# Attention into a leaky-ReLU MLP: a small memset behind GpSimd's copies, and an earlier place for one copy among VectorE's weight sums

## The chip, the cores and the metric

The kernel runs on one core of a Trainium2 chip. The metric is device time of one launch in microseconds (us). The engines are TensorE (PE, with its weight loads as PEld), VectorE (DVE), ScalarE (ACT), GpSimd (POOL) and SyncE (SP), each with a queue of its own that it works off in order; DMAs are issued from the queues of POOL (loads of the inputs) and SP (transposes and stores).

## The reference

```python
scores = scale * np.matmul(q, k.transpose(0, 1, 3, 2))      # q, k, v: 8 x 12 x 448 x 64, scale 1/8
scores = scores - np.max(scores, axis=-1, keepdims=True)
attn = np.exp(scores)
attn = attn / (np.sum(attn, axis=-1, keepdims=True) + 1e-09)
attn_out = np.matmul(attn, v)
x = attn_out.transpose(0, 2, 1, 3).reshape(3584, 768)
h = x @ w_in                                                # 768 x 2048
g = np.maximum(0.01 * h, h)
out = g @ w_out                                             # 2048 x 768
```

## The kernel before

**Pairs.** Attention is done for two heads at a time: pair u of 48, six pairs to a batch. A pair's q, k and v are loaded by DMA as bf16 into tiles `fq`, `fk`, `fv`, two pairs to a load, and copied by POOL (`cast`, L162 to L172): q and k into `qkb`, v into `v`, 112x512 each. For pairs up to 14, PE turns q and k (`transposes`, L248) into PSUM and DVE copies the result to `qkT` (L261); from pair 15 on (`NPE`) a DMA transpose from SP's queue does it (`turn`, L238). Then come four score chunks per pair (`scores`, L272, two matmuls each), an exponential on ACT for each chunk (L281), and `rows` (L755): 32 small matmuls (L764), the reciprocal of the sums (L770), and a scaled copy to `x` (L771), which is transposed to `xT` by DMA, in a few cases by PE (L318) with a copy by DVE (L319).

**The MLP.** The tokens are cut into seven blocks, of 640 first and 512 or so after that. Both weight products use a two-by-two scheme with seven products instead of eight, so sums of weight blocks are needed once and sums of data blocks for each token block. `mix_w_in` (L386, L390) and `mix_weights` (L364, L366, L369, L372) are generators: each `next` puts one sum of 128x768 bf16, with both inputs and the output in SBUF, into DVE's queue. `mix_weights` makes 16, in two halves of eight: for two pieces L364 then L366, then twice L369, then twice L372. L364 and L366 make `w_mix` 1 and 0, L369 changes `w_out_sb` in place, and L372 makes `w_mix` 2. `mix_h` (L435, L436) makes the same kind of sums of the hidden layer, `mix_x_part` (L415) of `xT`.

**Order.** [...] After the first batch's attention (`first`), `head` does the first 448 tokens' hidden layer, and `neck` (L609) the next 192, in eight groups; the function `after(x)` behind each group puts `mix_h` and some sums of `mix_weights` into DVE's queue. `second(0)` then does the first block's output product: `block_pair` (L518) yields after every four matmuls (L535), with DVE's work on `h` (L547, L552) and on the output (L540 copies a product from PSUM, L543 adds one). Into the gaps, `place` (L842) puts bursts of three score chunks and `rows`, by a small model of the engines' times in the program. In `second(0)` each second step also takes one more `next` of `mix_weights` if any is left. Later blocks are `hidden(i)` (L438) and `second(i)`, between which POOL's copies and load issues are given out by `advance` (L733); in the first phase this is done by `feed` (L822), from pair 12 on.

The product in `block_pair` that first reads `w_mix` is its third one, with `w_mix` 0 (t2 in the code); `w_out_sb` as changed by L369 is read by the fourth (t1), `w_mix` 1 by the fifth (t3), and `w_mix` 2 by the last (t4).

**Pair 14** is the last that PE turns. At the end of `neck` its turned q and k lie in a PSUM slot and wait for the copy L261:

```python
        after(len(ms) - 1)                       # neck: the last group's sums
...
    model["free"][id(slots[0])] = model["now"] + 1.5
    model["now"] += 0.45
    transposes(NPE - 1, next_slot()[:, 0])       # pair 14, ahead of second(0)
    to["pe"] += 1
    second(0)
```

`gate` is a 128x2 tile, written once at the start and used for nothing later.

Of the kernel before, what the change touches and what calls it, by code (L numbers as in the profile page):

```python
# [16 lines left out]
def kernel(  # L17
# [9 lines left out]
    nc = tc.nc  # L27
# [4 lines left out]
    HP = H // 2  # L32
# [34 lines left out]
    slots = [ps_s.tile([P, 2, 512], F32, name=f"sc{i}") for i in range(3)]  # L67

    def next_slot():

        slots.append(slots.pop(0))
        return slots[-1]

    def next_bank():

        banks.reverse()
        return banks[1]
# [17 lines left out]
    def place_of(t):  # L95
        return (t + NX - cuts[3]) % NX
# [65 lines left out]
    def cast(u, parts=(0, 1, 2), by=nc.gpsimd.tensor_copy):  # L162
        if u >= NU:
            return
        for x in parts:
            f = raw[u].pop(x)
            if x < 2 and u not in qk_sb:
                qk_sb[u] = cast_pool.tile([SC, 2, NSC, 2, D], BF16, name="qkb")
            if x < 2:
                by(qk_sb[u][:, x].rearrange("p so h d -> p h so d"), f)  # L170
            else:
                by(v_sb[u % NV][:, :, :, :D], f)  # L172

    w_steps = []
    for i in range(4):
# [26 lines left out]
    gate = const_pool.tile([P, 2], F32)  # L202
# [7 lines left out]
    def stay_warm(n):  # L210

        ps = next_slot()
        for _ in range(n):
            nc.tensor.matmul(ps[:, 0, :P], warm[:, :P], warm[:, :P], start=True, stop=True)
# [10 lines left out]
    def both(o, i):  # L225
        nc.scalar.copy(o[:, 0], i[:, 0])
        fast(o[:, 1], i[:, 1])

    cast(0, (1,), both)
    cast(0, (0,), both)  # L230


    x_t = {}

    NPE = HP + 9
# [8 lines left out]
    def turn_tile(bank):  # L244
        bank = next_bank() if bank is None else bank
        return bank.bitcast(BF16)[:, :2 * S].rearrange("p (i s) -> p i s", i=2)

    def transposes(u, bank=None):  # L248
        if u >= min(NPE, NU):
            return  # L250
        for parts in ((1,), (0,)) if u == 0 else ((0, 1),):
            tr = turn_tile(bank)
            for i in parts:
                for so in range(NSC):
                    nc.tensor.transpose(  # L255
                        tr[:, i, ts(so, SC)], qk_sb[u][:, i, so], ident[:SC, :SC]
                    )
            if u == 0:
                stay_warm(3 if parts == (1,) else 5)
            at = slice(parts[0], parts[-1] + 1)  # L260
            (nc.scalar.copy if u == 0 and parts == (1,) else nc.vector.tensor_copy)(  # L261
                qkT[u % NQ][:, :QL].rearrange("p (i s) -> p i s", i=2)[:, at], tr[:, at]
            )
# [73 lines left out]
    def settle():  # L337
        while late:
            expo(*late.pop(0))
# [88 lines left out]
    def mix_h(i, m):  # L428

        at = spots(i)[1]  # L430
        step = [max(1, at[-1][y] - at[0][y]) for y in range(2)]
        one, two = (slice(at[0][y], at[-1][y] + 1, step[y]) for y in range(2))
        lo, hi = slice(m, m + 2), slice(MH + m, MH + m + 2)
        t = h.rearrange("p m (c t) -> p m c t", t=P)
        nc.vector.tensor_sub(h_mix[:, lo, :len(at)], t[:, lo, one], t[:, lo, two])  # L435
        nc.vector.tensor_add(t[:, lo, two], t[:, lo, two], t[:, hi, two])  # L436
# [172 lines left out]
    def neck(outs):  # L609

        n = cuts[1] - HEAD
        at = place_of(HEAD)
        ms = [x + y for x in range(0, MH, 2) for y in (0, MH)]
        held = {}

        def part2(m, kks):
            fresh = m not in held
            if fresh:
                held[m] = next_bank()
            for j in range(2):  # L620
                for kk in kks:
                    nc.tensor.matmul(
                        held[m][:, j * n:(j + 1) * n], w_in_sb[:, kk, ts(m + j, P)], xT[:, kk, at:at + n],
                        start=(fresh and j == 0 and kk == 0), stop=(kk == KD - 1), skip_group_check=True,
                    )

        assert all(u == need[1] - 1 for u, _ in owed_x), owed_x
        def after(x):
            if x % 2:
                mix_h(0, ms[x - 1])  # L630
            for _ in range((1, 1, 1, 1, 1, 1, 2, 2)[x]):
                next(outs)

        for m in ms[:2]:
            part2(m, range(KD - 1))
        yield 4 * (KD - 1) * n / 2400, False
        for x, m in enumerate(ms):
            if x < 2:
                assert rows_done >= need[1], rows_done
                settle_x()  # L640
                part2(m, (KD - 1,))
                if x:
                    after(x - 1)
            else:
                part2(m, range(KH))
                after(x - 1)
                yield 2 * KH * n / 2400, False
                part2(m, range(KH, KD))
            nc.scalar.activation(
                h[:, m:m + 2, HEAD:cuts[1]], held.pop(m)[:, :2 * n].rearrange("p (m t) -> p m t", m=2), AX.Prelu, alpha=0.01  # L650
            )
            settle()
            yield 2 * (KH if x > 1 else 1) * n / 2400, True
        after(len(ms) - 1)

    def supply(u):

        for what, n in {0: [('qk', 2), ('qk', 3), ('v', 1), ('v', 2), ('load', 6)], 1: [('qk', 4), ('v', 3), ('load', 8)], 2: [('qk', 5), ('v', 4), ('w', 1)], 3: [('qk', 6), ('v', 5), ('w', 1)], 4: [('qk', 7), ('v', 6), ('load', 10)], 5: [('qk', 8), ('v', 7), ('w', 1), ('load', 12)]}[u]:
            if what == "qk":
                cast(n, (0, 1), fast if n in (2, 3) else nc.gpsimd.tensor_copy)  # L660
            elif what == "v":
                cast(n, (2,))
            elif what == "load":
                load(n)
            else:
                load_w(n)
# [132 lines left out]
    def settle_x(now=None):  # L799
        while owed_x and (now is None or owed_x[0][1] <= now and model["free"].get(id(slots[0]), 0.0) <= now + 0.05):  # L800
            model["free"][id(slots[0])] = model["now"] + 1.0
            model["now"] += 0.3
            x_transposes(owed_x.pop(0)[0], next_slot()[:, 0])
# [36 lines left out]
    model = {"now": 0.0, "act": 0.0, "free": {}, "ready": {}}  # L840
# [89 lines left out]
    for steps, aims, cost in ((head(ins, outs), early, 0.55), (neck(outs), goals, 0.5)):  # L930
        groups = 0
        base = len(early) if aims is goals else 0
        for used, full in steps:
            model["now"] += used
            if full:
                groups += 1
                model["act"] = max(model["act"], model["now"]) + cost
            soon = base + sum(x <= groups + 1 for x in aims) - done if full else 0
            done += place(0, base + sum(x <= groups for x in aims) - done, soon, first=True, lazy=True, full=full, keen=NU if aims is goals or groups > 13 else 0)
    settle()  # L940
    assert done == len(early) + len(goals), (done, chunk, rows_done)
    assert to["pe"] == NPE - 1, to
    model["free"][id(slots[0])] = model["now"] + 1.5
    model["now"] += 0.45
    transposes(NPE - 1, next_slot()[:, 0])
    to["pe"] += 1
    second(0)
    for _ in ins:
# [40 lines left out]
```

## Time and profile before

| | |
|---|---|
| median of 3 runs | 397.86 us (397.19 to 398.31) |
| the profiled execution | 398.14 us, span 396.4 us |
| PE busy | 380.4 us, 96% of the span |
| DVE busy | 236.8 us, 60% |
| ACT busy | 265.0 us, 67% |
| POOL busy | 140.0 us, 35%, 222 instructions |
| chain that ended last | PE 86%, DVE 5%, DMA 3%, issue 2%, ACT 2%, POOL 1% |

Times in the views are microseconds from the start of the span. A timeline line gives start, duration, engine, source line, operation, output tile and inputs, the shape, and in square brackets the idle time ahead of it and what ended it. Some neighbouring instructions of one kind are merged (x2, x32); back to back instructions overlap by some 0.06 to 0.08 us in the records. In the page, the row of busy tenths and that of the clock (PEclk) cut the span into 40 slices of 9.9 us.

### The profile page before, as it was taken

The numbers are of one execution on the slowest core, as the hardware profiler recorded it, in microseconds if no ns is written. First come the engines' busy times: TensorE is split into PE (matmuls) and PEld (weight loads), VectorE is DVE, ScalarE is ACT, GpSimd is POOL, SyncE is SP. The second block draws the span as 40 slices with busy tenths as digits, with TensorE's granted clock in tenths as the row PEclk, the third lists the DMA queues.
The fourth block names the chain that finished last, engine by engine and source line by source line (L and its number), as shares of the span: only waits on it lengthen the run. The fifth ranks groups of instructions, "written<-read, shape, count | busy, mean of one in ns | idle before, by whom it ended". The sixth has DMA issues, their size and how long they took to land.

```text
span 396.4 us, 10009 instructions
## 1 busy us (share of the span) xinstructions
PE 380.4 (96%) x4086; PEld 259.6 (65%) x4086; DVE 236.8 (60%) x494; ACT 265.0 (67%) x391; POOL 140.0 (35%) x222
## 2 busy tenths in 40 slices
PE   7899998759999999999999999999999999999996
PEld 3565656626659755697556975569755696568854
DVE  3653637973655854658448584464845656465754
ACT  6988874616587777677676776767767688708700
POOL 8897732934255321470216502265022200000000
PEclk9999999959999999999999999999999999999999
DMA  9999999994999918896398943989529520322023
GB/s 137 199 201 204 176 203 141 129 116 73 167 143 172 132 36 155 145 182 67 60 145 150 170 57 60 174 150 134 68 58 166 113 58 2 80 63 67 2 69 91
DMA packets 93246, 46.75 MB, mean 118 GB/s; under 512 B 51856, under 2 KB 89872, under 8 KB 93200
## 3 DMA queue, kind: packets, MB, share of 16 engines
q0 software_dynamic: 38224, 22.58, 45.2%
q1 hardware_dynamic: 54912, 23.50, 31.0%
q8 instruction: 32, 0.52, 0.6%
q14 instruction: 14, 0.11, 0.1%
q10 hardware_dynamic: 64, 0.02, 0.0%
HBM read 45.61 MB, written 11.01 MB: 143 GB/s over the span
## 4 chain that ended last, share of the span: by engine, by line
PE 86%; DVE 5%; DMA 3%; issue 2%; ACT 2%; POOL 1%; DVEq 0%; POOLq 0%; ACTq 0%
PE g L535 32%; PE g L463 13%; PE sc L463 13%; PE sc L764 11%; PE sc L272 9%; PE g L352 3%; PE g L291 2%; DMA w_in_mix<-in_k_dram 2%; DMA xT<-x 1%; ACT e L281 1%; PE g L255 1%; DVE w_mix L364 1%; POOL w_in_mix L141 1%; DVE w_mix L366 1%; PE sc L352 1%
## 5 line engine op out<-in xcount | busy, mean ns | idle before, releaser
L281 ACT ACTIVATE e<-sc 112x896 bf16<-112x896 f32 x192 | 162.7, 917 | 57.5 <-PE sc L272 57.3
L535 PEld LDWEIGHTS <-h 128*128 128x128 bf16 x680 | 61.9, 99 | 49.4 <-issue 15.5
L535 PE MATMUL g<-w_out_sb,h 128*128 128x384 bf16 x448 | 86.5, 332 | 0.0
L452 ACT ACTIVATE h<-c 128x512 bf16<-128x512 f32 (+1 forms) x72 | 43.5, 611 | 24.9 <-DVE c L478 16.2
L463 PEld LDWEIGHTS <-w_in_sb 128*128 128x128 bf16 x576 | 54.3, 98 | 6.0
L272 PE MATMUL sc<-qkT 64*128 64x448 bf16 x384 | 50.6, 358 | 7.6 <-DVE qkT L261 7.3
L764 PEld LDWEIGHTS <-e 112*128 112x128 bf16 x1344 | 46.6, 98 | 8.8 <-ACT e L281 7.2
L170 POOL COPY qkb<-fq 112x512 bf16<-112x512 bf16 x38 | 25.1, 660 | 77.2 <-DMA qkT<-qkb 44.8
L172 POOL COPY v<-fv 112x512 bf16<-112x512 bf16 x38 | 24.3, 643 | 75.3 <-PE sc L764 75.3
L764 PE MATMUL sc<-v,e 112*128 112x65 bf16 x1344 | 50.1, 194 | 0.6 <-ACT e L281 0.6
L463 PEld LDWEIGHTS <-w_in_mix 128*128 128x128 bf16 x432 | 41.2, 98 | 4.1
L535 PE MATMUL g<-w_mix,h 128*128 128x384 bf16 (+1 forms) x224 | 41.8, 324 | 0.0
L540 DVE COPY o<-g 128x384 f32<-128x384 f32 x53 | 29.3, 553 | 19.2 <-PE g L535 18.6
L272 PEld LDWEIGHTS <-qkT 64*128 64x128 bf16 x384 | 15.2, 94 | 34.0 <-issue 19.3
L770 DVE RECIPROCAL rec<-sc 112x8 f32<-112x8 f32 x42 | 8.7, 207 | 43.9 <-PE sc L764 43.6
L543 DVE TENSOR_TENSOR o<-o,g 128x384 f32<-128x384 f32 x42 | 23.2, 551 | 19.2 <-PE g L535 19.0
L170 POOL COPY qkb<-fk 112x512 bf16<-112x512 bf16 x38 | 25.4, 669 | 20.9 <-DMA fk<-in_k_dram 20.9
L771 DVE TENSOR_TENSOR x<-sc,rec 112x512 bf16<-112x512 f32 x42 | 29.0, 691 | 1.5
L463 PE MATMUL g<-xT,w_in_sb 128*128 128x256 bf16 (+1 forms) x216 | 28.5, 268 | 0.0
L463 PE MATMUL sc<-xT,w_in_sb 128*128 128x256 bf16 (+1 forms) x216 | 28.5, 268 | 0.0
L535 PE MATMUL g<-w_mix,hmix 128*128 128x384 bf16 x112 | 21.4, 327 | 0.0
L463 PE MATMUL g<-x_mix,w_in_mix 128*128 128x256 bf16 (+1 forms) x144 | 19.0, 268 | 0.0
(99 smaller groups left out, 460.1 us busy)
## 6 DMA issues: line engine op xcount, KB each, us to landing
fq<-in_q_dram POOLq DMA_DIRECT2D x19, 224.0 KB, 6.5
fk<-in_k_dram POOLq DMA_DIRECT2D x19, 224.0 KB, 8.3
fv<-in_v_dram POOLq DMA_DIRECT2D x19, 224.0 KB, 6.4
w_in_sb<-in_moe_w_in_dram POOLq DMA_DIRECT2D x4, 768.0 KB, 11.8
w_out_sb<-in_moe_w_out_dram POOLq DMA_DIRECT2D x4, 768.0 KB, 17.9
out_dram<-o SPq DMA_DIRECT2D x7, 336.0 KB, 3.9
out_dram<-o SPq DMA_DIRECT2D x8, 288.0 KB, 4.5
out_dram<-o SPq DMA_DIRECT2D x7, 240.0 KB, 3.3
```

Source lines behind the costliest of these rows:

```text
L170: by(qk_sb[u][:, x].rearrange("p so h d -> p h so d"), f)
L172: by(v_sb[u % NV][:, :, :, :D], f)
L272: nc.tensor.matmul(ps[:, j, :S], t[j * D:(j + 1) * D, S + c * SC:S + c * SC + P], t[j * D:(j + 1) * D, :S], start=True, stop=True,)
L281: nc.scalar.activation(e[:, :, c, :], sc_t.pop((u, c))[:SC, :, :S], AX.Exp, scale=scale)
L352: nc.tensor.matmul(open_t[m][:, :n], w_in_sb[:, kk, ts(m, P)], xT[:, kk, at:at + n], start=(fresh and kk == kks[0]), stop=(kk == KD - 1),)
L452: nc.scalar.activation(hs[:, m:m + 2, cols], x.rearrange("p (m t) -> p m t", m=2), AX.Prelu, alpha=0.01)
L463: nc.tensor.matmul(ps[:, j * nh:(j + 1) * nh], w[:, kk, ts(j, P)], x[:, kk], start=(first and j == 0 and kk == 0), stop=(kk == KH - 1), sk ...
L535: nc.tensor.matmul(ps[:, cols], x[:, m], w[:, m], start=(first and m == 0), stop=(m == MH - 1), skip_group_check=True,)
L540: by(o[:, at], ps[:, :NW])
L543: nc.vector.tensor_add(o[:, at], o[:, at], ps[:, :NW])
L764: nc.tensor.matmul(ps[:, j, qc, :], e[:, at:at + P], vt[:, j, c, :], start=(c == 0), stop=(c == NSC - 1),)
L771: nc.vector.tensor_mul(x_t[u].rearrange("p q j d -> p j q d"), ps[:SC, :, :, :D], rec.to_broadcast([SC, 2, NSC, D]))
```

## The change

Behind every copy that `cast` gives to an engine for pair 12 and later, POOL gets a memset of one column of `gate` (128x1, fp32): 108 of them. The turning of pair 14 and its copy to `qkT` move into `neck`, ahead of the last `after`. The last two calls of `after` take one sum of `mix_weights` each instead of two, so that two more are left to `second(0)`, one in each second step.

```diff
             else:
                 by(v_sb[u % NV][:, :, :, :D], f)
+            if u >= 2 * HP:
+                nc.gpsimd.memset(gate[:, :1], 0.0)
...
         def after(x):
             if x % 2:
                 mix_h(0, ms[x - 1])
-            for _ in range((1, 1, 1, 1, 1, 1, 2, 2)[x]):
+            for _ in range((1, 1, 1, 1, 1, 1, 1, 1)[x]):
                 next(outs)
...
             settle()
             yield 2 * (KH if x > 1 else 1) * n / 2400, True
+        model["free"][id(slots[0])] = model["now"] + 1.5
+        transposes(NPE - 1, next_slot()[:, 0])
         after(len(ms) - 1)
...
     assert to["pe"] == NPE - 1, to
-    model["free"][id(slots[0])] = model["now"] + 1.5
     model["now"] += 0.45
-    transposes(NPE - 1, next_slot()[:, 0])
     to["pe"] += 1
     second(0)
```

In the changed program DVE's order around the place is (old line numbers): L364, L770, L771, L435, L436, L366, L364, then L261 for pair 14, L435, L436, L366, L369, L547, L540, L369, L552, L543, L770, L771, L372, L540, L770, L771, L372. Before it was the same up to the second L364, then L366, L435, L436, L369, L369, L261, L372, L547, L540, L372, L552, L543. The orders of PE, ACT and SP are the same in both programs.

## The prediction

> **What bounds the kernel now.** I read the page first. TensorE (PE) is busy 96% of the span, so time can only come from its idle time or from its clock, and the clock row has one low digit, in the ninth slice (79 to 89 us).
>
> ```profile
> PE   7899998759999999999999999999999999999996
> PEclk9999999959999999999999999999999999999999
> ```
>
> Second, PE's waits, summed over the run. One of them (7.3 us in all, 6.6 the longest) outweighs the rest together:
>
> ```profile
> PE sc L272 <- DVE qkT L261: 7.3, 3, 6.6
> ```
>
> Third, PE's timeline there, and the windows around it (busy time of PE, PEld, DVE, ACT, POOL, then granted clock):
>
> ```profile
> 75.50 0.82 PE L535 MATMUL g<-w_out_sb,h 128*128 128x384 bf16 x4
> 76.25 0.55 PE L272 MATMUL sc<-qkT 64*128 64x448 bf16 x4
> 83.43 0.55 PE L272 MATMUL sc<-qkT 64*128 64x448 bf16 x2 [6.63 <-DVE qkT L261]
> 83.91 4.02 PE L535 MATMUL g<-w_out_sb,h 128*128 128x384 bf16 x12
> ```
>
> ```profile
> 76.80:79.25 2.45, 0.00 (x0) 0.00 (x0) 2.42 (x4) 1.64 (x2) 2.45 (x4) 1.00 1.13 127
> 79.25:83.43 4.18, 0.00 (x1) 0.01 (x2) 4.08 (x7) 0.00 (x0) 2.37 (x4) 0.50 1.73 138
> 83.43:89.49 6.06, 6.06 (x22) 2.25 (x23) 3.33 (x6) 1.88 (x3) 1.17 (x2) 0.50 0.54 95
> ```
>
> PE stops at 76.80 for 6.63 us, because the third score chunk of the burst needs pair 14's turned q and k. 2.45 us into the stop the clock halves, and stays so until 89.49: the 12 L535 matmuls take 4.02 us (0.32 apart, against 0.163 at full clock). Full speed began at 4.16, ended at 79.25 and returned at 89.49; 75.09 and 10.24 us are 22 and 3 times 3.413 us, so the clock is decided in steps of 3.413. The stop therefore costs 6.63 us and half of 6.06, 9.66 in all. After 89.49 PE has no gap over 0.3 us.
>
> Fourth, why the copy is late: VectorE (DVE) and GpSimd (POOL) at that place.
>
> ```profile
> 71.39 4.11 DVE L364 TENSOR_TENSOR w_mix<-w_out_sb 128x768 bf16<-128x768 bf16 x1
> 75.42 0.20 DVE L770 RECIPROCAL rec<-sc 112x8 f32<-112x8 f32 x1
> 76.25 0.42 DVE L435 TENSOR_TENSOR hmix<-h 128x512 bf16<-128x512 bf16 x1
> 77.34 0.97 DVE L366 TENSOR_TENSOR w_mix<-w_mix,w_out_sb 128x768 bf16<-128x768 bf16 x1
> 79.22 1.40 DVE L366 TENSOR_TENSOR w_mix<-w_mix,w_out_sb 128x768 bf16<-128x768 bf16 x1
> 81.40 1.43 DVE L369 TENSOR_TENSOR w_out_sb<-w_out_sb 128x768 bf16<-128x768 bf16 x2
> 82.76 0.61 DVE L261 COPY qkT<-sc 128x896 bf16<-128x896 bf16 x1
> ```
>
> ```profile
> 71.70 0.62 POOL L172 COPY v<-fv 112x512 bf16<-112x512 bf16 x1
> 72.25 0.62 POOL L170 COPY qkb<-fq 112x512 bf16<-112x512 bf16 x1
> ...
> 74.48 0.60 POOL L170 COPY qkb<-fk 112x512 bf16<-112x512 bf16 x1
> 75.03 0.70 POOL L141 DMA_DIRECT2D fq<-in_q_dram  x1
> 77.11 0.77 POOL L172 COPY v<-fv 112x512 bf16<-112x512 bf16 x1
> ```
>
> L364 takes 0.55 us elsewhere (61.88 and 64.24) and 4.11 here, while six copies run back to back, 0.555 apart; it ends 0.47, its own length, after the last one starts to give way at 75.03. It is not w_out's load: the last was issued at 42.7 and none took over 22.4 us to land. So an operation with two SBUF inputs was held for 3.56 us by a train of copies. From 77.11 to 79.6 the two engines take turns instead (copies of 0.77, 0.94, 0.93; sums of 0.97, 0.96), and one sum (1.40) waits for two copies. The trace does not say why one train lets DVE in and the other not.
>
> **The change, part by part.** The order of PE, ACT and SP is unchanged, instruction for instruction. DVE's queue changes between the second-last L364 pair and the second output block; POOL's gains 108 memsets (36 pairs, three copies each).
>
> Pair 14's copy moves. It was behind L366, L435, L436 and two L369; now it follows L364 at once. By the rows, L364 ended at 79.19, the copy started at 82.76: 3.57 us. Moved behind it: L435, L436, L366 (a third product's weights, w_mix 0), L369, and, past L547, L540, L552, L543 and a row pair's L770 and L771, the other L369 and both L372. Their readers: L369's result is read at 92.6 and L372's at 99.2, over 5 us after their new places; nothing there is late. L366 and L435 to L540 are read by the product at 89.11, which is next in line (below).
>
> The memsets' own price. The four 128x1 memsets at the start (L973) start 0.04, 0.03 and 0.04 apart: 0.035 each. All but the first wait for POOL's own earlier memset, which a copy of 0.555 separates from them. The upper bound is the row of DMA issues that wait for POOL's own copy (L141 behind L172: 1.2 us in 4 times), 0.30 each. I take 0.04, as the wait is long satisfied. A train of six gains 0.24 (at most 1.8). Queued behind it: casts, load issues and, through the casts, SP's transposes. Cover: from a k copy's end to that pair's first score the tightest later pair, 20, has 18.1 us (96.65 to 114.75), and transposes are issued 9 us or more ahead of use.
>
> What a memset may bring: a moment without a reading POOL instruction, in which a waiting DVE sum gets in. Taking turns, as from 77.11 on, is the row nearest to this; the train at 71.70 is the other bound. I take turns. Then L364 starts at 72.25 and ends at 72.72. L770 must wait for its matmuls (72.10 plus 1.19) and starts at 73.36; with L771 (0.22 and 0.61 between starts) 74.20. L435, L436, L366, L364 at 0.52, 0.52, 0.47, 0.47 make 1.98, and two copies' waits of 0.5 about 1.0 more: 77.15. The qkT copy of 0.55 ends near 77.7, PE resumes at 77.75. Saved: 83.43 less 77.75, 5.68; ends: 6.63 (no gap) and 2.9 (a copy ahead of each of the five). A stop of 0.95 is below the 2.45 in which the clock was taken, and stops of 0.76 and 0.64 (62.85, 67.51) did not lose it: 3.03 more.
>
> What is late next: PE's w_mix product. PE reaches it at 77.75 + 0.48 (two scores) + 12 × 0.163 + 0.67 (six scores) = 80.85. DVE must first do L435, L436, L366, L369, L547, L540: 0.52 + 0.52 + 0.47 + 0.47 + 0.61 + 0.47 = 3.06 from 77.70, 80.76, and it meets the next train of copies (the one of 77.11): three or four waits of 0.5, so 82.3 to 82.8. I take a stall of 1.7 (0 without copies, 2.5 with one ahead of every sum). Net 5.68 + 3.03 − 1.7 = 7.0. The profiled execution took 398.14 (span 396.4 and 1.7 around it): 391.1. The median of the runs is 0.28 lower: 390.9.
>
> **Where the skill speaks against it.** The Trainium skill, SBUF — State Buffer, section Who interferes with whom, says that the second input of such a sum comes through a read interface shared with GpSimd, that whoever starts first has it for one instruction, and that an instruction that only writes does not contend. By that alone L364 would have lost one copy, 0.56, and the train needs no memset; the trace's 3.56 decides against it. By the rule the kernel would gain only from the moved copy.
>
> TensorE: Matmul & The Clock Gate, Part 1, has about one busy window of 3.4 us bring full speed back; here PE worked 6.06 us at half clock first, since its first 3.413 step was not fully busy. By the rule the recovered clock would be worth 1.7 and the total 392.2.
>
> **Rivals.** (1) The memset opens nothing: the train holds L364 as before. Six memsets push it 0.24; from L364's end to the second L364's end is 75.50 to 79.19 in the rows, so the qkT copy ends about 80.0 and PE resumes at 80.05. Saved 3.4. The clock halves at 79.25 all the same; the first full 3.413 step is then 82.66 to 86.08, and 6.03 us run at half clock: nothing won there. 394.5. For it: six copies without a break; against it: turns taken at 77.8 and 78.7.
>
> (2) Given back later: the xT transposes of 108.75 take 5.63 us to land and the sums behind them end at 118.06 for a product at 119.76. If the loads between 99 and 115 (146 GB/s) set that time rather than PE, up to 6 us return: about 397. Against it: those loads are issued behind v copies that wait for PE (75.3 us in 14 waits), and the DMA share is 0.02 from 89.49 to 93.
>
> (3) Slower: a memset is dear. Its place is POOL's queue in each 49.3 us stage (pair 21's first score to pair 27's), with 18 copies (0.555) and 9 issues (0.70), 16.3 us. It decides once memset plus copy fill the stage: (49.3 − 16.3) / 18 = 1.8 us each. At 2.0 a stage takes 52.3, 3 us more in each of five, less the 7.0: 406. Only a cost six times the 0.30 bound does it.
>
> **How the numbers follow.** Turns taken: 0.59, with a range of its own of 388.2 (no gap, no stall) to 393. Rival 1: 0.24. Rival 2: 0.07, mostly within 0.3% (1.2 us, about what a measurement of this kernel can tell from no change). Rival 3, or a milder form of it: 0.10. The range 388.6 to 395.3 takes in the first but its edge, and rival 1 with the 0.24 to 1 us that its memsets may cost. Faster 0.85, same 0.05, slower 0.10.
>
> **What would show it.** Right: in the after profile L366 (the old L364) at 71.4 takes about 1.3 us, the qkT copy ends before 78.5, PE's stop is under 2 us, no low digit in PEclk, and a new wait of PE's w_mix product for DVE of 1 to 2 us near 81. Rival 1: 4 us for that sum and a low digit that stays. Rival 2: PE waits for xT or x_mix near 109. Rival 3: memsets far over 0.3 us, PE waits for qkT transposes. The forecast is wrong if the stop shrinks as said and the end does not move with it.

## The result, and the profile after

The changed kernel takes 393.23 us (median of 4 runs, 392.24 to 393.66) against 397.52 before: a ratio of 0.9891, 95% interval 0.9857 to 0.9924. Faster, as forecast, by 4.3 us where 7.0 were forecast (390.9, from the 397.86 then known). The profiled execution took 392.24 us, span 390.4. In the changed program line numbers are higher by 2 to 4 (the old L364 is L366, L435 is L437, L261 is L263, L535 is L537). Each later ratio is of means, to the kernel before in the same rounds, and leaves out one execution each of two kernels that took far longer than the others (396.45 and 2125.08 us), which the medians include.

The profile that follows is of one of the best executions. The mean granted clock is on record for each: 1.00 in two of ten of the changed kernel (this one and one of 392.03 us; six of the ten were taken later), 0.989 to 0.995 in the other eight.

The clock row of the page, after:

```profile
PEclk9999999999999999999999999999999999999999
```

PE's timeline at the place:

```profile
78.94 0.36 PE L274 MATMUL sc<-qkT 64*128 64x448 bf16 x2 [1.74 <-DVE qkT L263]
83.32 0.81 PE L537 MATMUL g<-w_mix,h 128*128 128x384 bf16 x4 [1.28 <-DVE o L542]
```

The stop of 6.63 us is 1.74, the clock stays up in this execution, and a new wait of 1.28 us stands ahead of the product with `w_mix`. That product starts at 83.32 instead of 89.11, 5.8 us earlier; the span is 6.0 us shorter. So what the place gave arrived at the end.

The same stretch of DVE and of POOL:

```profile
72.39 0.55 DVE L366 TENSOR_TENSOR w_mix<-w_out_sb 128x768 bf16<-128x768 bf16 x1
74.64 2.23 DVE L437 TENSOR_TENSOR hmix<-h 128x512 bf16<-128x512 bf16 x1
78.26 0.62 DVE L263 COPY qkT<-sc 128x896 bf16<-128x896 bf16 x1
```

```profile
73.05 0.63 POOL L172 COPY v<-fv 112x512 bf16<-112x512 bf16 x1
...
75.41 0.60 POOL L170 COPY qkb<-fq 112x512 bf16<-112x512 bf16 x1
75.96 0.09 POOL L174 MEMSET gate<- 128x1 f32 x1
76.00 0.60 POOL L170 COPY qkb<-fk 112x512 bf16<-112x512 bf16 x1
```

A memset costs 0.04 us between copies, as forecast. But it lets nobody in: the sum L437 met the train at 74.64 and got through only behind its last copy (it ended at 76.87; less its own 0.35, which is its usual 0.42 without the overlap of the records, that is 76.52, and the last copy ran from 76.00 to about 76.55). L366 took its normal 0.55: it began at 72.39 and was through when the train began at 73.05. Before, the sum's record began at 71.39 and the train at 71.70, inside the 0.55 us that the sum needs. The train had moved, not opened.

### The profile page after: what moved, and what is told of

It reads as the page before. It is cut to its first block, busy times and chain, and to the rows that moved or that the text cites. A ratio compares the mean times of both kernels' runs of the same rounds, so it can differ in the third digit from the quotient of the medians.

```text
span 390.4 us, 10108 instructions
## 1 busy us (share of the span) xinstructions
PE 378.1 (97%) x4086; PEld 259.3 (66%) x4086; DVE 235.0 (60%) x494; ACT 265.2 (68%) x391; POOL 143.4 (37%) x330
## 4 chain that ended last, share of the span: by engine, by line
PE 87%; DVE 4%; DMA 4%; ACT 2%; issue 1%; POOL 1%; DVEq 0%; POOLq 0%; ACTq 0%
PE g L537 31%; PE g L465 14%; PE sc L465 14%; PE sc L768 11%; PE sc L274 9%; PE g L354 3%; DMA xT<-x 2%; DMA w_in_mix<-in_k_dram 2%; PE g L293 2%; PE g L624 1%; ACT e L283 1%; PE g L257 1%; DVE hmix L437 1%; POOL w_in_mix L141 1%; PE sc L354 1%
## 5 line engine op out<-in xcount | busy, mean ns | idle before, releaser
L537 PEld LDWEIGHTS <-h 128*128 128x128 bf16 x680 | 61.3, 98 | 49.0 <-issue 13.8
L537 PE MATMUL g<-w_out_sb,h 128*128 128x384 bf16 x448 | 84.6, 326 | 0.0
L170 POOL COPY qkb<-fq 112x512 bf16<-112x512 bf16 x38 | 24.2, 637 | 78.5 <-DMA fq<-in_q_dram 40.4
L537 PE MATMUL g<-w_mix,h 128*128 128x384 bf16 (+1 forms) x224 | 41.6, 323 | 1.3 <-DVE o L542 1.3
L170 POOL COPY qkb<-fk 112x512 bf16<-112x512 bf16 x38 | 26.5, 697 | 17.4 <-DMA fk<-in_k_dram 17.4
L537 PE MATMUL g<-w_mix,hmix 128*128 128x384 bf16 x112 | 21.4, 327 | 0.0
L465 PE MATMUL sc<-x_mix,w_in_mix 128*128 128x256 bf16 (+1 forms) x144 | 19.0, 268 | 0.0
```

Of the source, the lines that this page charges most:

```text
L465: nc.tensor.matmul(ps[:, j * nh:(j + 1) * nh], w[:, kk, ts(j, P)], x[:, kk], start=(first and j == 0 and kk == 0), stop=(kk == KH - 1), sk ...
L537: nc.tensor.matmul(ps[:, cols], x[:, m], w[:, m], start=(first and m == 0), stop=(m == MH - 1), skip_group_check=True,)
```

## The experiments

Four explanations were set against each other; "held" means that a sum of VectorE's takes several times its usual time while GpSimd copies. **A**, the forecast: a memset lets a waiting sum in. **B**: the memset does nothing, and the moved copy is the gain. **C**: a train behind a DMA issue can hold a sum to its end, because GpSimd's cores are then out of step and the shared port is never free; only a memset that must wait for the memset just ahead of it restores step. **D**: any sum that meets a train is held, by chance.

**The two parts alone, and the full change once more.** Memsets alone, on the kernel before:

```diff
                 by(v_sb[u % NV][:, :, :, :D], f)
+            if u >= 2 * HP:
+                nc.gpsimd.memset(gate[:, :1], 0.0)
```

> The memsets alone, DVE's order as before. Theory A (the memset lets a waiting sum in): the sum that took 4.11 us takes at most 1.3, pair 14's copy ends about 3 us earlier, PE's stop is 3 to 4 us instead of 6.6; about 394.5. Theory B (the memset opens nothing; the moved copy is the whole gain, and where the train of copies falls among the sums is chance): the same as before within 0.3%, 396.5 to 398.5, with one DVE sum of 2 us or more inside a train that now has 0.04 us memsets in it.

Measured: 397.48 us, ratio 0.9995 (0.9977 to 1.0013). From its profile, DVE, POOL and PE:

```profile
70.81 3.96 DVE L438 TENSOR_TENSOR h<-h 128x512 bf16<-128x512 bf16 x1
```

```profile
73.89 0.60 POOL L170 COPY qkb<-fk 112x512 bf16<-112x512 bf16 x1
74.43 0.09 POOL L174 MEMSET gate<- 128x1 f32 x1
```

```profile
83.07 0.56 PE L274 MATMUL sc<-qkT 64*128 64x448 bf16 x2 [6.11 <-DVE qkT L263]
```

Six copies, each with its memset, hold a sum from 70.8 to 74.4, and PE stops for 6.1 us, much as before. The move alone, that is pair 14's copy and the spread sums:

```diff
-            for _ in range((1, 1, 1, 1, 1, 1, 2, 2)[x]):
+            for _ in range((1, 1, 1, 1, 1, 1, 1, 1)[x]):
...
+        model["free"][id(slots[0])] = model["now"] + 1.5
+        transposes(NPE - 1, next_slot()[:, 0])
         after(len(ms) - 1)
```

> The moved copy of pair 14 and the spread sums, no memsets. Theory A: PE's stop stays at 3 us or more, because the train still holds a sum for 3.5 us; about 394.5. Theory B: as the full change, 393.2 within 0.3%; a sum is held by the train for 2 to 4 us in the profile just as in the full change.

Measured: 392.14 us, ratio 0.9867 (0.9845 to 0.9889). Its DVE line and its PE line:

```profile
69.84 3.84 DVE L435 TENSOR_TENSOR hmix<-h 128x512 bf16<-128x512 bf16 x1
```

```profile
79.83 0.56 PE L272 MATMUL sc<-qkT 64*128 64x448 bf16 x2 [3.01 <-DVE qkT L261]
80.32 3.35 PE L535 MATMUL g<-w_out_sb,h 128*128 128x384 bf16 x12
```

The hold is there, the stop is 3 us, the clock halves for one step only, and the kernel is as fast as with the memsets. (The profile is of the slowest of its five executions, 393.26 us.) The full change once more:

> The full change once more, on the chip and in the rounds of the two parts. Both theories: 392.2 to 394.0, a ratio near 0.989. In the profile, theory A wants no sum above 1.3 us between 69 and 83 us; theory B wants one of about 2 to 4 us in a train.

Measured: 393.55 us, ratio 0.9903 (0.9869 to 0.9937). In this profiled execution (395.58 us) one sum was held for 4.24 us (71.39) and another for 1.99 (77.38), PE stopped for 3.95, and the clock was at half for two steps (79.53 to 86.35): the same program, 3.3 us slower than in its first profiled execution. What differs between the two profiles is which sums the trains met. A falls, B holds for the times. The two kernels' intervals overlap, so whether the memsets cost anything is not resolved.

**The hold by itself.** A kernel without attention or MLP runs trains of six copies and lets off one subtraction at the second copy's end:

```python
if dma:
    nc.gpsimd.dma_start(out=ld, in_=...)      # 112 x 4 x 256
for i in range(6):
    nc.gpsimd.tensor_copy(dst[i], src)
    for _ in range(memsets):
        nc.gpsimd.memset(gate[:, :1], 0.0)
nc.vector.tensor_sub(s, dst[1], b)            # waits for the second copy
```

> No attention and no MLP: eighteen trains of six 128x512 bf16 copies on GpSimd, each with 0, 1 or 3 memsets behind a copy, with and without a DMA issue just ahead; the second copy's end lets off one DVE subtraction of 512 columns with two SBUF inputs (0.33 us by itself as an estimate from 0.42 for 512 columns in the profile). Theory A: with one memset the subtraction takes under 1.0 us. Theory B: with no memset and with one it takes 2 us or more (held to the train's end, four copies of 0.555), at least behind a DMA issue; with three memsets, each of which waits for the one before, it gets in at the next copy's end and takes under 1.2 us.

Measured, from DVE's timeline (one line for each kind behind a DMA issue with 0, 1 and 3 memsets, then one without an issue and with 1):

```profile
9.27 1.90 DVE L41 TENSOR_TENSOR s<-dst,b 128x512 bf16<-128x512 bf16 x1 [2.34 <-POOL dst L37]
18.49 2.59 DVE L41 TENSOR_TENSOR s<-dst,b 128x512 bf16<-128x512 bf16 x1 [2.25 <-POOL gate L39]
29.55 0.43 DVE L41 TENSOR_TENSOR s<-dst,b 128x512 bf16<-128x512 bf16 x1 [2.62 <-POOL gate L39]
43.86 0.83 DVE L41 TENSOR_TENSOR s<-dst,b 128x512 bf16<-128x512 bf16 x1 [1.29 <-POOL gate L39]
```

Behind an issue: 1.90, 0.80, 2.45 without memsets; 2.59, 2.59, 2.59 with one; 0.43, 0.42, 0.43 with three. With no issue ahead: 0.36, 0.87, 0.80 and 0.43, 0.83, 0.83 with none and one (0.42, 0.43, 0.42 with three). So with one memset behind each copy the sum was held in every train behind an issue; without an issue no sum waited for more than one copy. The expected 2 us or more without memsets came in one train of three (2.45; the others 1.90 and 0.80). A second kernel of this kind put memsets ahead of the first copy instead (0, 1 or 2), two behind each copy, or one input in PSUM, all behind an issue:

> No attention and no MLP: fifteen trains of six copies, each right behind a DMA issue; the second copy's end lets off one DVE subtraction. Theory C: with nothing between, and with one memset ahead of the first copy, the subtraction is held to the train's end or near it (about 2 us or more in most trains); with two memsets ahead, the second waiting for the first, it takes under 1.0 us; with two behind each copy under 0.6; with one input in PSUM instead of SBUF it is not held at all, about 0.4 to 0.6.

Measured: nothing between: 0.80 and 0.80 (the first train, at the start, 0.36); one ahead: 0.80, 1.90, 0.80; two ahead: 0.80 three times; two behind each: 0.43, 0.43, 0.42; one input in PSUM: 0.69 three times. The expectation that most trains without a pair of memsets hold failed: 2 of 3 did in the first kernel, 1 of 5 here. No train with a pair held it (9 of 9, at most 0.80). But this does not yet speak for C. With two or three memsets behind each copy the copies start 0.76 or 0.90 us apart instead of 0.555, and the sum can run in that pause, in step or not; and with two ahead the sum took the 0.80 that it took with nothing between. The PSUM form takes 0.69 every time, more than the 0.4 to 0.6 expected, but the length that L771's 512 columns take in the kernel with no copy near (60.51 us before), so it was not held.

**Memsets that wait, in the kernel.** Three memsets behind each copy of the full change:

```diff
-                nc.gpsimd.memset(gate[:, :1], 0.0)
+                for _ in range(3):
+                    nc.gpsimd.memset(gate[:, :1], 0.0)
```

> The full change with three memsets instead of one behind each copy, each of which must wait for the one before to be done. Theory C (a copy train right behind a DMA issue never leaves the shared port free, since GpSimd's parts are out of step after the issue; a memset that waits for the memset just before it brings them back in step, one that does not wait changes nothing): no DVE sum between 68 and 83 us above 1.5 us, PE's stop under 2 us, the clock stays, about 390.5. Theory D (any DVE sum that meets a train is held by chance): a hold of 2 us or more as in the full change, 392 to 394.

Measured: 389.63 us, ratio 0.9815 (0.9789 to 0.9841). DVE's sum that was held before, and PE:

```profile
71.62 0.96 DVE L367 TENSOR_TENSOR w_mix<-w_out_sb 128x768 bf16<-128x768 bf16 x1
```

```profile
77.58 0.36 PE L275 MATMUL sc<-qkT 64*128 64x448 bf16 x2 [0.54 <-DVE qkT L264]
```

The longest sum between 68 and 83 us takes 1.09, one copy's wait; the stop is 0.54 and the clock does not fall (the mean granted clock is 1.00 in four of five executions). Here too the copies are 0.90 us apart, so a pause alone could explain it. The next kernel has no pause in the train: only two memsets stand between a DMA issue and the first copy behind it, with the move and with nothing behind the copies (the comments in this cut are added here):

```diff
+    skew = []
...
+        skew.append(u)                        # in load_soft: a load was issued
...
+            if u >= 2 * HP and skew:          # in cast, ahead of the copy
+                skew.clear()
+                for _ in range(2):
+                    nc.gpsimd.memset(gate[:, :1], 0.0)
```

> The moved copy and spread sums; no memset behind copies, but two memsets between a DMA issue of GpSimd and the first copy behind it, from pair 12 on, the second of which waits for the first. Theory C: the trains start in step, so a sum waits for one copy at most (0.9 to 1.1 us for a sum of 0.55); PE's stop under 2 us, about 390.5. Theory D: a hold of 2 to 4 us stays, about 392.

Measured: 390.57 us, ratio 0.9823 (0.9801 to 0.9845), a granted clock of 1.00 in all five executions; no stop ahead of the scores, and

```profile
80.98 0.81 PE L542 MATMUL g<-w_mix,h 128*128 128x384 bf16 x4 [1.01 <-DVE o L547]
```

The same pair of memsets with nothing moved:

> The kernel before with nothing moved, and the two memsets between a DMA issue of GpSimd and the first copy behind it, from pair 12 on. Theory C: the 4 us hold is gone, so pair 14's copy, though still behind all its sums, ends about 3.5 us earlier, near 79.5; PE's stop about 3 us; 393.5 to 394.5, a ratio near 0.991: the hold and the place of the copy share the loss. If the hold never mattered with the copy in its old place: 397.5.

Measured: 394.49 us, ratio 0.9932 (0.9909 to 0.9955). Its longest sum between 68 and 83 us takes 0.96, pair 14's copy ends at 80.75 (79.5 expected) and PE still stops 3.64 (3 expected). So by these ratios the hold alone is worth 0.7%, the move with the spread sums 1.3%, both 1.8%.

**The move taken apart.** Only pair 14's turning and copy moved, the sums not spread:

> Only pair 14's turning and copy are moved; the sums of w_out stay two behind each of the last two groups, no memsets. If the place of the copy is the whole gain: as with the spread sums, 392.1 within 0.3%. If the spread matters, PE waits longer ahead of the first w_mix product, as L366 and a second L369 come before L547 and L540: 0.5 to 1 us more, 392.6 to 393.2.

Measured: 395.07 us, ratio 0.9942 (0.992 to 0.9963), slower than expected by 2 us. The expectation put a loss, if any, ahead of the `w_mix` product; it arose ahead of the copy, because the second-last `after` then still takes two sums, so that one more stands ahead of it.

```profile
79.88 0.85 DVE L366 TENSOR_TENSOR w_mix<-w_mix,w_out_sb 128x768 bf16<-128x768 bf16 x1
80.65 0.61 DVE L261 COPY qkT<-sc 128x896 bf16<-128x896 bf16 x1
```

The copy starts at 80.65 (79.17 with the spread sums), and the stop is 3.89.

**Pair 14 copied by ScalarE.** In the move alone, without memsets:

```diff
-            (nc.scalar.copy if u == 0 and parts == (1,) else nc.vector.tensor_copy)(
+            (nc.scalar.copy if u == 0 and parts == (1,) or u == NPE - 1 else nc.vector.tensor_copy)(
```

> The moved copy and spread sums without memsets, and pair 14's turned q and k copied by ScalarE instead of DVE. If DVE's queue ahead of that copy is what PE stops for, the stop ahead of the scores is under 0.3 us and the clock stays, whatever the train holds; PE then waits ahead of the first product with w_mix, for the same DVE sums, 2.5 to 4 us. Theory C and D alike: about 391, a hold of 2 to 4 us still in DVE's line. If ScalarE is late for its exponentials through the copy: 393.

Measured: 392.81 us, ratio 0.9888 (0.9866 to 0.9911), 1.8 above the 391 expected, and near the 393 expected if ScalarE were late through the copy.

```profile
83.54 1.44 PE L535 MATMUL g<-w_mix,h 128*128 128x384 bf16 x4 [3.34 <-DVE o L540]
```

The stop went, and the held sums (4.12 us for one) made PE wait 3.34 us at the next place instead; that wait took the clock too (1.44 us for four matmuls, 0.81 elsewhere), which the expectation had left out. ScalarE was not what PE waited for: it was idle for 0.37 us at 79.55, waiting for PE's scores, while PE stopped from 80.20. With the pair of memsets as well:

> Both: pair 14 copied by ScalarE, and the two memsets ahead of a first copy. Theory C: no stop ahead of the scores, under 1.5 us ahead of the first w_mix product, clock kept: 388.5 to 389.5, faster than both kernels. Theory D: as with ScalarE's copy alone, about 391.

Measured: 389.81 us, ratio 0.9824 (0.9797 to 0.9851); the wait there is 0.34. That is a little above the 388.5 to 389.5 expected, and not shown to be faster than the two others: the three kernels with waiting memsets and pair 14 moved have overlapping intervals. All three have their upper bound below the lower bound of the full change's first measurement; against the move alone (0.9845 to 0.9889) only three memsets are clear of it.

Over its whole span, each of the seven profiles without a waiting memset has a bf16 sum of 2.23 to 4.24 us with both inputs in SBUF; in the four with them the longest takes 1.31. That does not fit D. Whether the pair helps only by moving the train 0.26 us later was not tested apart; against it, the sums of these four meet the trains at different places, and none takes over 1.31.

## Why the prediction was right, and where it was not

**The place, the cause and the sign** were right: PE's one long stop, the two-input sum held by a train of copies, the clock lost with it, and nothing given back later. But the gain came from the moved copy, and not from the memsets that the sum was built on: the sign was right by the change's other half. No run shows PE waiting for an xT or qkT transpose behind the place, and the dear memset (rival 3) is excluded by 0.04 us in the trace.

**What failed is one step, "I take turns".** The memset was taken to open the train, and weighed at 0.59 against 0.24 for rival 1, in which it opens nothing. The memsets alone do nothing (0.9995), so rival 1 had the mechanism. The rows that were used for turns (77.11 to 79.6) showed only that trains sometimes give way; the trace did not say why, and the forecast should have weighed the row at the very train concerned, 3.56 us, at least as high. In the first profile after, PE resumed at 78.94 where 77.75 was forecast: 4.49 us saved of 5.68, 3.03 for the clock and 1.28 lost in the stall, 6.2 in all for a span 6.0 shorter. In the second PE resumed at 81.31 and the clock fell; that the clock term was won whole is the exception among the ten executions.

**Where the sums get in, the forecast's arithmetic holds.** With three memsets PE resumed at 77.58 (forecast 77.75), the clock stayed, and the net gain came to 0.0185 × 397.5 = 7.4 us (forecast 7.0). The stall at the `w_mix` product, taken at 1.7, was 1.28 in the changed kernel, 1.01 with the pair of memsets, and nearly gone with three, where the next copies come later: mis-sized, with the right sign. One bound of the forecast was added up wrongly: the 2.9 us for a copy ahead of each of five is 5.68 less five copies of 0.555, but the 5.68 already had two of them off; off the 6.63 without gaps they leave 3.9.

**Rival 1's sum was right in its times and wrong in its clock.** It had PE resume at 80.05 and the clock win nothing: 394.5. The move alone resumed at 79.83 and took 392.14 (its profiled execution 393.26). Three windows, each one clock step of 3.41 us long: before, the move alone, and pair 14's copy on ScalarE (the stretch, its length, PE's busy time first, the granted clock behind the five engines):

```profile
82.66:86.08 3.42, 2.65 (x9) 1.14 (x10) 1.84 (x4) 0.92 (x1) 1.59 (x3) 0.50 1.28 213
79.44:82.86 3.42, 3.02 (x11) 1.27 (x11) 3.07 (x7) 0.92 (x1) 1.84 (x3) 0.50 1.23 187
82.97:86.38 3.41, 2.84 (x33) 2.27 (x34) 2.05 (x5) 0.00 (x0) 1.57 (x2) 0.50 0.97 151
```

Before, a step with PE busy 2.65 of 3.42 us (77%) did not bring the clock back, nor did 2.72 of 3.41 (80%) with the memsets alone (82.38 to 85.79). In the move alone PE was idle for some 0.4 us of the step, and full speed returned at its end, 82.86; with ScalarE's copy 2.84 of 3.41 (83%) was enough. The forecast had asked for a fully busy step. So PE worked 3.03 us at half speed in the move alone, at a cost of 1.5 us instead of 3.0. How much it costs depends on where the steps fall, which differs from run to run; whether that makes the spread of single runs was not tested apart.

**One copy or a whole train.** The Trainium skill, SBUF — State Buffer, section Who interferes with whom, has whoever starts first hold the shared ports for one instruction. The trains without an issue ahead agree (at most 0.87 us for a sum of 0.43); behind an issue they do not (2.59, four copies), so the measurement decides. That a sum with one input in PSUM is not held (0.69) agrees with its rule on two SBUF inputs.

**What stays open.** The Trainium skill, GPSIMD Engine Reference, section Instruction dispatch, says that GpSimd's eight cores each start the next instruction when done with their own share of the last one, with nothing but an instruction's own doing to synchronise them, and that a wait on the completion holds back what must come after; this is where C came from. That they are out of step behind an issue is an inference: it fits that the holds stood behind an issue and that no hold is in a profile with waiting pairs, but no view shows the cores. Why 3 of 8 such trains without a pair behind the copies held a sum in the small kernels (counting one memset ahead as none), while holds of 3.8 to 4.2 us stand in six of the seven profiles of full kernels without a pair, was not settled; nor why the train of 77.11 before, also behind issues, let sums in. In those six the held sum's record begins 0.13 to 0.32 us ahead of the train's first copy; whether it had begun to read is not shown. And one execution of the kernel with three memsets (396.45 us, granted clock 0.986) and one of that with nothing moved (398.58, 0.983) took as long as the kernel before; neither has a profile, so whether a hold came back in them is open.

## What to carry to other kernels

Where a DVE operation with two SBUF inputs takes several times its usual time, lay it beside GpSimd's line: a train of copies right behind a DMA issue can hold it to the train's end, and a single cheap instruction behind each copy changed nothing (0.9995), while two small ones between the issue and the first copy, the second waiting for the first, cost some 0.3 us, and no profile with them has a hold. Copies that TensorE waits for belong ahead of sums that nobody needs yet; count what is still ahead of them in the queue, sum by sum. A forecast for one profiled execution holds the luck of its queues: look at a second one before building on the exact order of two engines that nothing ties together.

## What the runs showed of the hardware that was not expected

A one-column memset behind each copy, in a train behind a DMA issue, held DVE in 3 of 3 trains (2.59 us), against 2 of 3 with no memset in the same kernel (1.90 and 2.45): it did not help. A pair of dependent one-column memsets took 0.28 us in the timeline. PE's clock came back after steps of 3.41 us with 83% and 88% of busy time, and not after steps with 77% and 80%. The hold lies inside the record of the sum (4.11 us for 0.55), with no wait shown ahead of it.
